# Keeping GpSimd's recorded order at the start of the main phase of a graph tensor product, with a wider window for one sort and edge numbers unpacked one unit later

## The chip, the cores and the metric

The kernel runs on one core of a Trainium2 chip. The metric is the device time of one execution in microseconds (us). The engines are PE (TensorE, matmuls; PEld is its weight load), DVE (VectorE), ACT (ScalarE), POOL (GpSimd) and SP (SyncE, which here only issues DMAs). L1043 means line 1043 of the kernel before the change.

## What is computed

There are N = 10000 nodes with 64 channels of 4 components each, and E = 640000 edges with random source and destination nodes. Each edge takes its source node's row of x, combines it with its own direction Y by the small tensor cg, scales it by a learned radial factor and adds the result to its destination node. At the end a 64 x 64 matrix mixes the channels.

```python
R = _silu(edge_feat @ w_rad)                              # (E, C)
xs = x[src]                                                 # (E, C, M)
tp = jnp.einsum('eci,ef,ifo->eco', xs, Y, cg)             # (E, C, M)
msg = R[:, :, None] * tp
agg = _segment_sum(msg.reshape(-1, C * M), dst, N).reshape(N, C, M)
return jnp.einsum('ncm,cd->ndm', agg, w_mix)
```

## The kernel before

The edges are sorted by destination on the chip, so that the messages of 32 neighbouring nodes can be summed by matmuls. The 32 nodes are a *bucket*, 18 buckets are a *group* (the last group has 7), and the edges are cut into three *parts* (32, 36.4 and 31.6 per cent). One part of one group is a *segment*; there are 3 x 18 = 54 of them, in the order of the list `self.segs`, which begins each part with the short group. The first segment therefore has 7 buckets, the second 18.

The first phase sorts part 0 by groups into DRAM. The main phase (`groups`) does three things at once:

- `messages` computes the messages. Its work is cut into 939 *units*, one bucket of one part each (5 or 6 tiles of 128 edges). A loop over k runs a pipeline of stages; `(gather, LG)` in its table means that the gather of unit k+5 stands in step k. `index` (L991 to L1000) takes the edge numbers `sidx` of a whole segment out of the sorted words `pay` on DVE, LI units ahead, at the first unit of each segment. `gather` (L1043) fetches 5 or 6 tiles of rows of x by indirect DMAs on POOL, five units ahead, into `xg`, which has seven buffers. `turn`, `turned`, `radial` and `silu` make the radial factors; `products` (L1096, DVE) multiplies `xg` by them, and `sums` (L1109, PE) adds a unit's messages up.
- `pass2` sorts one segment after the other by buckets. A segment is routed in *chunks* of 13 tiles: DVE makes `X` (L649), ACT and DVE make `oh`, PE multiplies them into the one PSUM bank `pr` (L682, L685), ACT copies the bank to `rt` (L690, five buffers), and POOL stores it with one indirect DMA, `bkt<-rt` (L696). While a segment is routed, `front` makes the tables of the next one. After the last chunk SP loads the segment's words back as `pay`, two buffers of them.
- `pass1` sorts the later parts by groups; its stores are `grp<-rt`.

`groups` weaves the three. A step v is a *quarter*: one of the four groups of stages of one unit. Segment i+1 must be sorted by quarter `ends[i]`; its sort is spread evenly from the end before. PE, DVE and ACT keep the order in which the instructions are recorded (`manual_schedule`). POOL and SP do not: a list scheduler with a cost model orders them at build time, and the engine then runs that order strictly.

```python
quarters = (((index, LI), (gather, LG), (fetch, 1), (turn, 2), (sums, 0), (silu, 1), (piece(0), 5), (piece(1), 4),
             (piece(2), 3)), ((evict, -1), (turned, 2), (spots, 1)),
            ((products, 1), (rest(0), 5), (rest(1), 4)), ((radial, 2), (full, -1)))
...
for k in range(-LI, n + 3):
```

Unit u is therefore gathered in step u-5 and multiplied in the third quarter of step u-1, and its segment's numbers are taken out in step u-LI. As step -LI is quarter 0, `index` of unit u always stands in quarter 4u, while everything else of `messages` moves by four quarters when LI moves by one.

Of the kernel before, what the change touches and what calls it, by code (L numbers as in the profile page):

```python
# [37 lines left out]
UT = 6  # L38
SPLIT = ((0.32, 5), (0.364, 6), (0.316, 6))
LG = 5  # L40
LI = 8
HEAVY = 4
BIG = 16384.0
FAR = 2097152.0
# [18 lines left out]
def weave(main, side, ratio):  # L63

    acc = 0.0
    for said in main:
        acc += ratio
        while acc >= 1.0:
            acc -= 1.0
            next(side, None)  # L70
        yield said
    yield from side


def run(gen):
    for _ in gen:
        pass


class Kernel:  # L80
# [868 lines left out]
    def messages(self):  # L949
# [63 lines left out]
        def piece(q):  # L1013
            def cast(k):

                at = block(k)
                if at is None:
                    return
                key, v, n = at
                if q == 0:  # L1020
                    E9[key] = ph.tile([P, HB * MT, 3, 3, 4], BF, name="e9", bufs=2)
                    ER[key] = ph.tile([P, HB * MT, 4], F, name="er", bufs=1)
                r = ER[key][:, :n] if q else v
                nc.scalar.activation(E9[key][:, :n, :, q, :], r.unsqueeze(2).to_broadcast([P, n, 3, 4]), AF.Copy)
            return cast
# [132 lines left out]
        def mixed(k, po):  # L1158
# [4 lines left out]
# [4 lines that stand above are left out]
        todo, po = [], None  # L1167
        for k in range(-LI, n + 3):
            for stages in quarters:
# [15 lines left out]
    def groups(self):  # L1185

        self.pay = {}
        sort, main, segs, NG = self.pass2(), self.messages(), self.segs, self.NG

        ends, u = [], 0  # L1190
        for k, g in segs:
            u += self.nb(g)
            ends.append(4 * max(u - LI - 3, ends[-1] // 4 + 1 if ends else 1))

        for k in range(1, len(SPLIT)):
            ends[k * NG - 1] -= 22

        later, at = [], 40
        for k in range(1, len(SPLIT)):
            end = max(ends[k * NG - 2] - 8, at + 1)  # L1200
            n = self.chunks(k)
            later.append((self.pass1(k, self.p1.NC // 2 * 2), at, end, HEAVY * n + 20 * (n / (self.p1.NC - 2) + 2)))
            at = end
        done = 0.0
        while segs[0] not in self.pay:
            next(sort)
        batch, got = self.batch(), None
        acc = 0.0
        i = start = 0
        for v in range(4 * u):  # L1210

            if later:
                first, at, end, n = later[0]
                due = "grp" in (self.held, self.pos, self.way)
                while done < n * (v + 1 - at) / (end - at) or due:
                    due = False
                    said = next(first, "end")
                    if said == "end":
                        later.pop(0)
                        done, self.sorted = 0.0, self.sorted + 1  # L1220
                    if said in ("held", "end"):
                        break
                    done += said or 1
            if i + 1 < len(segs):
                acc += self.pass2_steps(*segs[i + 1]) / (ends[i] - start)
                due = "bkt" in (self.held, self.pos, self.way)
                while (acc > 0.0 or v >= ends[i] or due) and segs[i + 1] not in self.pay:
                    due = False
                    said = next(sort)
                    if said == "held":  # L1230
                        break
                    acc -= said or 1
                if v >= ends[i] and segs[i + 1] in self.pay:
                    i, start, acc = i + 1, ends[i], 0.0
            elif got is None:
                if segs[-1] in self.pay:
                    run(sort)
                    self.remains()
                    got = "begun"
            elif got != "ready":  # L1240
                got = next(batch) or got
            next(main)
        assert not later
        for _ in main:
            if got != "ready":
                got = next(batch) or got
        while got != "ready":
            got = next(batch) or got
        run(batch)

    def chunks(self, part):
# [246 lines left out]
    def add(self, pay, si, dst, wx):  # L1498

        al = lambda nm, shape: self.ph.tile(shape, F, name=nm, bufs=1 + (nm == "oeq"))  # L1500
        xg = al("oxg", [P, OT, 64, 4])
        di = self.ph.tile([P, OT], I32, name="odi")
        self.reach(xg, si)
        run(self.join(al, pay, dst, di, [xg], wx))
        self.put(al, di, [xg])
# [37 lines left out]
    def run(self):  # L1543
        tile_pool, nc = self.tc.tile_pool, self.nc
        order = [self.NG - 1] + list(range(self.NG - 1))
        self.segs = [(k, g) for k in range(len(SPLIT)) for g in order]
        with tile_pool(name="p1", bufs=2) as self.ph, tile_pool(
                name="x1", bufs=1, space=bass.MemoryType.PSUM) as self.px:
            self.ways = 2
            self.rt_bufs, self.ls = 38, 8  # L1550
            self.lag, self.ahead, self.early = 2, 3, 1
            self.z = self.ph.tile([P, 2048], F, name="z", bufs=1)
            nc.gpsimd.memset(self.z, 0.0)
            self.consts()

            with self.tc.manual_schedule(engines={mybir.EngineType.SP}):
                first = self.pass1(0, 8)
                next(first)
                run(self.clear_groups(0, nc.gpsimd))
                for _ in range(40):  # L1560
                    next(first, None)
                while self.held:
                    next(first)
                self.weights()
                later = itertools.chain(self.clear_buckets(),
                                        *(self.clear_groups(k, nc.sync) for k in range(1, len(SPLIT))))
                run(weave(first, later, 0.185))
                self.sorted = 1
        with tile_pool(name="p2", bufs=2) as self.ph, tile_pool(
                name="x2", bufs=1, space=bass.MemoryType.PSUM) as self.px:  # L1570
            self.ways = 1
            self.rt_bufs, self.ls = 5, 4
            self.lag, self.ahead, self.early = 1, 2, 0
            self.p1.NC = 13
            self.p1.act = self.p2.act = 7
            with self.tc.manual_schedule(engines={mybir.EngineType.PE, mybir.EngineType.DVE,
                                                  mybir.EngineType.Activation}):
                self.groups()
        with tile_pool(name="p3", bufs=1) as self.ph, tile_pool(
                name="x3", bufs=1, space=bass.MemoryType.PSUM) as self.px:  # L1580
            self.ways = 2
            self.rest()
# [29 lines left out]
```

## Time and profile before

| what | us |
|---|---|
| time, median of 3 runs | 9988.29 |
| lowest and highest of these | 9968.19, 9993.34 |
| profiled execution, its own time | 9898.0 |
| its span, first to last instruction | 9896.2 |
| busy in the span: PE, DVE, ACT, POOL | 6566.6, 6947.1, 4425.9, 5961.4 |

The profiled execution is 0.9% faster than the median of the three runs, so durations are added up against 9898.0 and the result is carried over to the median by proportion. No engine is busy all the time: DVE leads with 70% of the span. In rows of the timeline the first number is the start in us from the span's start, the second the duration; `[14.01 <-remote]` is the engine's idle time before the instruction and what ended it. "issue" means that nothing shown ended the wait, "remote" that a semaphore did whose sender the profile cannot name. The starts and ends of matmuls are modelled.

### The profile page before, as it was taken

To read this page: it belongs to the slowest core of one execution; us is meant where nothing else is said; L and a number is where in the kernel's file an instruction comes from. 1 tells how busy PE (TensorE), PEld (TensorE's weight loads), DVE (VectorE), ACT (ScalarE), POOL (GpSimd) and SP (SyncE) were. 2 spreads that over 40 slices of the span, in tenths; PEclk is the share of its full clock that TensorE was granted. 3 is DMA by queue.
4 is the path that set the end of the run, shared out by engine and by line. 5 is a ranking of instruction groups with operands and counts; after the bars stand their busy time and mean duration, and the time that the engine had idled before them with its cause. 6 is when DMAs were issued, how large, how long until landed. Compare 5 with 4: busy or idle time off the path is not lost. (4 is left out here: it accounts for less than half of the span.)

```text
span 9896.2 us, 126276 instructions
## 1 busy us (share of the span) xinstructions
PE 6566.6 (66%) x41310; PEld 5222.8 (53%) x41310; DVE 6947.1 (70%) x13605; ACT 4425.9 (45%) x12394; POOL 5961.4 (60%) x6213
## 2 busy tenths in 40 slices
PE   6646666666666666666666666666666676667666
PEld 4435555555555555455555554555555555555555
DVE  8868878787876767767777777556666656666554
ACT  6845555555655444544544444433232323333221
POOL 4546666666666566566666666666556555555555
PEclk6568888887888777777777787777777777877878
DMA  6223333333333333333333333334334343344433
GB/s 206 85 63 101 102 102 100 102 103 101 99 103 101 97 108 104 94 105 102 101 103 105 98 101 101 100 107 112 111 111 119 107 120 112 112 116 114 115 108 94
DMA packets 694112, 1050.60 MB, mean 106 GB/s; under 512 B 272066, under 2 KB 501826, under 8 KB 693440
## 3 DMA queue, kind: packets, MB, share of 16 engines
q0 software_dynamic: 289104, 741.62, 26.3%
q1 hardware_dynamic: 404336, 300.81, 10.4%
q8 instruction: 325, 5.32, 0.2%
q14 instruction: 347, 2.84, 0.1%
HBM read 841.68 MB, written 213.95 MB: 107 GB/s over the span
## 5 line engine op out<-in xcount | busy, mean ns | idle before, releaser
L1043 POOL DMA_INDIRECT xg<-in_x_dram,sidx x5165 | 4934.7, 955 | 3054.0 <-issue 1354.6
L1109 PE MATMUL G<-S,xg 128*128 128x128 f32 x20660 | 3220.9, 315 | 550.4 <-issue 529.0
L1109 PEld LDWEIGHTS G<-S,xg 128*128 128x128 f32 x20660 | 2980.0, 226 | 639.1 <-issue 621.5
L682 PE MATMUL pr<-X,oh 128*128 128x320 bf16 (+2 forms) x10538 | 1888.6, 341 | 1083.5 <-ACT rt L690 486.6
L682 PEld LDWEIGHTS <-oh 128*128 128x128 bf16 x10538 | 1162.5, 117 | 1777.5 <-issue 1083.0
L1096 DVE TENSOR_TENSOR xg<-xg,pre 128x1536 f32<-128x1536 f32 (+1 forms) x939 | 1516.0, 1614 | 626.0 <-ACT pre L1072 421.7
L649 DVE TENSOR_TENSOR X<-dv,Wt 128x2080 f32<-128x2080 f32 (+4 forms) x854 | 1668.0, 1953 | 330.3 <-remote 216.8
L673 ACT ACTIVATE sq<-far,rowf 128x128 f32<-128x128 f32 x5702 | 1754.2, 394 | 2.7
L1072 ACT ACTIVATE pre<-pre 128x384 f32<-128x384 f32 (+1 forms) x939 | 423.6, 451 | 2042.2 <-issue 768.6
L1082 DVE TENSOR_TENSOR S<-dv,pay 128x768 f32<-128x768 f32 (+1 forms) x939 | 836.6, 891 | 510.3 <-remote 318.8
L674 ACT ACTIVATE oh<-sq,ones 128x896 bf16<-128x896 f32 (+2 forms) x854 | 899.9, 1054 | 23.9
L690 ACT ACTIVATE rt<-pr 128x320 bf16<-128x320 f32 (+1 forms) x854 | 349.5, 409 | 1197.2 <-remote 810.2
L696 POOL DMA_INDIRECT bkt<-rt,idx x437 | 439.3, 1005 | 409.3 <-issue 104.9
L1068 PE MATMUL pre<-wr,sT 108*128 108x192 bf16 x939 | 262.3, 279 | 634.1 <-ACT sT L1061 399.1
L1061 ACT ACTIVATE sT<-pre 108x256 bf16<-108x256 f32 x939 | 358.7, 382 | 531.9 <-remote 258.5
L1134 DVE TENSOR_TENSOR Gs<-old,G 128x256 f32<-128x256 f32 x313 | 130.3, 416 | 653.8 <-remote 410.1
L1154 PE MATMUL po<-wf,Gs 128*128 128x256 f32 (+2 forms) x1392 | 416.1, 454 | 138.4 <-ACT tot L433 83.3
L1068 PEld LDWEIGHTS <-sT 108*128 108x128 bf16 x939 | 98.3, 105 | 752.3 <-ACT sT L1061 453.5
L1056 PE MATMUL pre<-identb,e 128*108 128x128 bf16 x1878 | 305.8, 250 | 249.1 <-DVE xg L1096 160.2
L1056 PEld LDWEIGHTS <-e 128*108 128x108 bf16 x1878 | 247.5, 152 | 392.3 <-issue 301.3
L665 DVE TENSOR_TENSOR oh<-dv,pair 128x768 bf16<-128x768 bf16 (+3 forms) x852 | 446.8, 525 | 0.2
L1154 PEld LDWEIGHTS po<-wf,Gs 128*128 128x128 f32 (+2 forms) x1392 | 297.1, 220 | 228.1 <-ACT tot L433 86.5
(317 smaller groups left out, 6644.4 us busy)
## 6 DMA issues: line engine op xcount, KB each, us to landing
xg<-in_x_dram,sidx POOLq DMA_INDIRECT x5165
sums<-Gp SPq DMA_DIRECT2D x626, 128.0 KB
old<-sums SPq DMA_DIRECT2D x313, 256.0 KB
bkt<-z SPq DMA_DIRECT2D x26, 990.0 KB
pay<-bkt SPq DMA_DIRECT2D x68, 225.0 KB
ye<-in_Y_dram SPq DMA_DIRECT2D x103, 96.0 KB
ye<-in_edge_feat_dram SPq DMA_DIRECT2D x103, 96.0 KB
grp<-z SPq DMA_DIRECT2D x17, 580.0 KB
```

Of the source, the lines that this page charges most:

```text
L649: nc.vector.tensor_tensor(X[:, :m, :].rearrange("p t (s w) -> p t s w", w=W), msk.unsqueeze(3).to_broadcast([P, m, ps.r, W]), QD[c // Q][1 ...
L665: nc.vector.tensor_tensor(oh[:, :v, :].rearrange("p t (h k) -> p t h k", k=2), self.vb.rearrange("p (h k) -> p h k", k=2).unsqueeze(1).to_ ...
L673: nc.scalar.activation(sq[:, u, :], self.far, AF.Square, bias=to, scale=-1.0)
L674: nc.scalar.activation(oh[:, v:v + len(at), :], sq[:, :len(at), :], AF.Relu, bias=self.ones[:, 0:1], scale=-2.0)
L682: nc.tensor.matmul(pr[:, o:o + 2 * ps.rw], oh[:, u, :], X[:, u, :].bitcast(BF), start=(u == 0), stop=(not on and (u == m - 1 or u % TT == ...
L696: st = nc.gpsimd.indirect_dma_start(out=ps.dst, out_offset=bass.IndirectOffsetOnAxis(ap=idx[:, i:i + 1], axis=0), in_=rt[:, s * ps.rw:(s + ...
L1043: nc.gpsimd.indirect_dma_start(out=xg[:, t, :], out_offset=None, in_=self.x, in_offset=bass.IndirectOffsetOnAxis(ap=si[:, u:u + 1], axis=0))
L1056: nc.tensor.matmul(pre[:KR, 256 + 128 * h:384 + 128 * h], e[:, 36 * t:36 * t + KR], self.identb, start=True, stop=True)
L1082: nc.vector.tensor_tensor(S[:, :ut], self.eq[:, :ut].unsqueeze(3).to_broadcast([P, ut, NB, 4]), pb[:, :, 1:5].unsqueeze(2).to_broadcast([P ...
L1096: nc.vector.tensor_tensor(V, V, R.unsqueeze(3).to_broadcast([P, ut, 64, 4]), op=OP.mult)
L1109: nc.tensor.matmul(G[:, h].rearrange("p n f -> p (n f)"), v[:, 32 * h:32 * h + 32, :].rearrange("p c i -> p (c i)"), s.rearrange("p n f -> ...
L1154: nc.tensor.matmul(po[:nn, :256], Gs[:, h, f].rearrange("p b n -> p (b n)")[:, :nn], self.wf[:, h, f, :], start=(h + f == 0), stop=(h + f ...
```

## The change

Three edits, all in or for `groups`. LI goes from 8 to 7, so `index` stands seven units ahead. The first end, for the second segment's sort, becomes quarter 20 instead of quarter 4; the other ends stay, as the formula now has 11 where it had LI + 3. And `groups` yields once, at quarter 28, so that its caller can record everything up to there with POOL, too, in the recorded order.

```diff
-LI = 8
+LI = 7
...
-            ends.append(4 * max(u - LI - 3, ends[-1] // 4 + 1 if ends else 1))
+            ends.append(4 * max(u - 11, ends[-1] // 4 + 1 if ends else 5))
...
         for v in range(4 * u):
-
+            if v == 4 * LI:
+                yield
...
-            with self.tc.manual_schedule(engines={mybir.EngineType.PE, mybir.EngineType.DVE,
-                                                  mybir.EngineType.Activation}):
-                self.groups()
+            kept = {mybir.EngineType.PE, mybir.EngineType.DVE, mybir.EngineType.Activation}
+            groups = self.groups()
+            with self.tc.manual_schedule(engines=kept | {mybir.EngineType.Pool}):
+                next(groups)
+            with self.tc.manual_schedule(engines=kept):
+                run(groups)
```

On POOL, the main phase begins with the stores of the first segment's four chunks. In the order before, this follows (`xg<-in_x_dram` are gathers, five for each unit; `bkt<-rt` stores of one chunk each, eight for each whole segment of the first part):

```order
L696 DMA bkt<-rt,idx 136704x160 x4
L1043 DMA xg<-in_x_dram,sidx 128x256 x10
L696 DMA bkt<-rt,idx 136704x160
L1043 DMA xg<-in_x_dram,sidx 128x256 x8
L696 DMA bkt<-rt,idx 136704x160
L1043 DMA xg<-in_x_dram,sidx 128x256 x15
L696 DMA bkt<-rt,idx 136704x160
L1043 DMA xg<-in_x_dram,sidx 128x256 x2
L696 DMA bkt<-rt,idx 136704x160 x9
L1043 DMA xg<-in_x_dram,sidx 128x256 x5
```

On POOL at the same place, now:

```order
L696 DMA bkt<-rt,idx 136704x160 x4
L1043 DMA xg<-in_x_dram,sidx 128x256 x5
L696 DMA bkt<-rt,idx 136704x160 x2
L1043 DMA xg<-in_x_dram,sidx 128x256 x5
L696 DMA bkt<-rt,idx 136704x160 x3
L1043 DMA xg<-in_x_dram,sidx 128x256 x5
L696 DMA bkt<-rt,idx 136704x160 x3
L1043 DMA xg<-in_x_dram,sidx 128x256 x25
L696 DMA bkt<-rt,idx 136704x160
L1043 DMA xg<-in_x_dram,sidx 128x256 x5
```

Before, 35 gathers (units 0 to 6) stand around the first three of the second segment's eight stores; now 15 do, and units 3 to 7 follow the eighth store in one run of 25.

On DVE, the first `index` stands, before, behind the third segment's digits and the first `X` (L649) of the second segment; the rows begin with the places (`pair`, `slot`) of the second segment's first chunks:

```order
L633 TENSOR_SCALAR pair<-pos 128x104
L636 SCALAR_TENSOR_TENSOR slot<-pair,pos 128x52
L646 TENSOR_TENSOR dv<-dv,slot 128x208
L649 TENSOR_TENSOR X<-dv,Wt_7625 128x2080
L1276 TENSOR_TENSOR unp<-pay,sh 128x280
L1278 SCALAR_TENSOR_TENSOR pay<-unp,pay 128x35x8
L991 TENSOR_SCALAR sidx<-pay 128x35
```

On DVE now (line numbers behind L1193 are higher by one to four), the same `index` follows the first two rows on the third segment's words (L885, L886), ahead of its digits (L375, L381):

```order
L885 TENSOR_SCALAR dg_7892<-Wt_7888 128x102
L886 TENSOR_SCALAR dg_7892<-dg_7892 128x102
L1277 TENSOR_TENSOR unp<-pay,sh 128x280
L1279 SCALAR_TENSOR_TENSOR pay<-unp,pay 128x35x8
L991 TENSOR_SCALAR sidx<-pay 128x35
L993 TENSOR_SCALAR didx<-pay 128x35
L1000 SCALAR_TENSOR_TENSOR dlc<-didx,bn 128x35
L375 TENSOR_SCALAR two<-dg_7892 128x204
L381 TENSOR_TENSOR D_7895<-dv,two 128x720
```

So 10 rows of DVE (of L375, L381, L627, L633, L636, L646 and L649, the first `X` among them) that stood ahead of the first `sidx` now stand behind it. From unit 5 on, DVE's products stand between the sorts' rows as they stood before, but for one unit: what unit u had before it, unit u+1 now has (all but 14 of them, which differ by one chunk); PE's and ACT's rows do so from unit 11 on at the latest. Each `index` stands between the same sort rows as before, and so one product later.

## The prediction

> **What bounds the kernel now.** No engine is busy all the time, so I looked first for stretches in which none is, in the table of windows at the start of the main phase, the only place where the two kernels' POOL orders differ much. The numbers after each window's length are busy time and count by engine, then the granted PE clock, the DMA share and GB/s:
>
> ```profile
> core 0: us, PE busy (x) PEld busy (x) DVE busy (x) ACT busy (x) POOL busy (x), PEclk, DMA share, GB/s
> 575.00:600.00 25.00, 9.84 (x50) 5.49 (x49) 20.71 (x53) 12.84 (x35) 13.65 (x15) 0.64 0.23 66
> 600.00:625.00 25.00, 3.99 (x15) 2.02 (x15) 6.14 (x7) 4.05 (x11) 18.84 (x21) 0.57 0.36 102
> 625.00:650.00 25.00, 12.87 (x63) 7.33 (x63) 12.82 (x28) 16.10 (x43) 6.73 (x7) 0.70 0.12 34
> 650.00:675.00 25.00, 15.86 (x85) 8.90 (x85) 21.62 (x52) 15.36 (x44) 3.94 (x4) 0.79 0.18 47
> 656.00:762.00 106.00, 67.86 (x428) 53.16 (x426) 85.67 (x194) 52.10 (x149) 51.49 (x54) 0.79 0.32 89
> ```
>
> From 600 to 625 us DVE works 6.14 of 25 us and PE 3.99, while POOL issues. The waits of ACT between 575 and 640 us (total, times, longest) name the place, the copy of `pr` to `rt`:
>
> ```profile
> ACT rt L690 <- remote: 35.8, 2, 21.8
> ```
>
> The timeline of that stretch shows a chunk's last matmul early, and its copy late:
>
> ```profile
> 574.63 0.21 DVE L886 TENSOR_SCALAR dg<-dg 128x102 int32<-128x102 int32 x1
> ...
> 578.54 2.32 DVE L649 TENSOR_TENSOR X<-dv,Wt 128x2080 f32<-128x2080 f32 x1
> ...
> 582.08 1.00 POOL L1043 DMA_INDIRECT xg<-in_x_dram,sidx  x1 [10.72 <-DVE didx L993]
> ...
> 587.15 0.94 POOL L1043 DMA_INDIRECT xg<-in_x_dram,sidx  x1 [0.30 <-issue]
> 587.18 2.32 DVE L649 TENSOR_TENSOR X<-dv,Wt 128x2080 f32<-128x2080 f32 x1
> 589.00 0.30 PE L685 MATMUL pr<-rt,oh 128*128 128x320 bf16 x1
> ...
> 605.34 0.44 ACT L690 ACTIVATE rt<-pr 128x320 bf16<-128x320 f32 x1 [14.01 <-remote]
> ...
> 609.24 0.41 PE L685 MATMUL pr<-rt,oh 128*128 128x320 bf16 x1
> ...
> 613.63 0.95 POOL L1043 DMA_INDIRECT xg<-in_x_dram,sidx  x1 [0.30 <-issue]
> ...
> 624.89 0.95 POOL L1043 DMA_INDIRECT xg<-in_x_dram,sidx  x1 [0.30 <-issue]
> 631.25 0.44 ACT L690 ACTIVATE rt<-pr 128x320 bf16<-128x320 f32 x1 [21.83 <-remote]
> ```
>
> The second and third chunk of the second segment are copied 16 and 22 us after their last matmuls start (589.00 to 605.34, 609.24 to 631.25). Since there is only one `pr`, PE's next chunk waits too, then DVE. POOL issues gathers nearly without a pause from 582.08 to 624.89, and the wait ends 6 us after the last. That coincidence is all the trace says of the cause: `rt` has five buffers, which should not bind here, and the wait's sender is not named. Taking the stalls for the gathers' doing is the choice on which the forecast rests.
>
> **The change part by part.** It adds and removes no work: equally many gathers, stores, products and sort rows. I follow three positions in DVE's order, from which the rest is carried on unchanged: the second segment's last `X`, the first product, and a product behind the third segment's sort.
>
> ```profile
> 646.71 1.99 DVE L649 TENSOR_TENSOR X<-dv,Wt 128x1760 f32<-128x1760 f32 x1
> 648.73 0.34 SPq L869 DMA_DIRECT2D Wt<-gr  x1
> 652.27 0.25 DVE L885 TENSOR_SCALAR dg<-Wt 128x102 int32<-128x102 int32 x1 [3.16 <-DMA Wt<-gr]
> ...
> 656.61 2.33 DVE L649 TENSOR_TENSOR X<-dv,Wt 128x2080 f32<-128x2080 f32 x1
> ...
> 680.41 1.48 DVE L1096 TENSOR_TENSOR xg<-xg,pre 128x1280 f32<-128x1280 f32 x1
> ...
> 761.97 1.48 DVE L1096 TENSOR_TENSOR xg<-xg,pre 128x1280 f32<-128x1280 f32 x1
> ```
>
> *The second segment's sort.* Its last `X` stands at 646.71. Now three units' gathers stand around its stores instead of seven, in fives with two or three stores between; that is the pattern of one unit's gathers per chunk or two that the rest of the main phase has. I take both stalls away: 35.8 us. The ends are nothing gone, and 35.8; I stand at the upper one, because the run of 33 gathers (582.08 to 624.89, broken by two stores) no longer exists there: 15 are left, and none between the last three stores.
>
> *`index` ahead of the digits.* It now waits for `pay` before DVE has ten rows to hide the load under. The load is issued after this row:
>
> ```profile
> 572.93 0.50 SPq L933 DMA_DIRECT2D pay<-bkt  x1
> ```
>
> The nearest load on the same queue is that of `Wt`, issued at 648.73 and used at 652.27, 3.5 us. So `pay` is there at about 576.6 at the earliest, and DVE is free at 574.63 + 0.21 = 574.84: 1.8 us of waiting, with ACT, PE and the next tables behind it; the ends are 0 and twice the wait, 3.6. The last `X` then stands at 646.71 - 35.8 + 1.8 = 612.7.
>
> *The first product.* Everything of the messages stands one unit earlier against the sort, so unit 0's product now stands ahead of the third segment's first `X`. From the last `X` to that `X` is 656.61 - 646.71 = 9.9 us, most of it the load of `Wt`, which does not change; I allow 9.4 to the product's start, as it takes the place of that `X`'s last wait: 622.1, against 680.41 before. The product needs unit 0's gathers, which are the first five on POOL from about 582 on.
>
> *The third segment's sort.* From its first `X` (656.61) to the product of unit 10 (761.97) there are 105.4 us with eight chunks and 11 units. The same rows now lie between the products of units 0 and 11. DVE is busy for 85.67 of this (the window from 656 to 762); the rest has more of the same wait:
>
> ```profile
> 706.14 0.44 ACT L690 ACTIVATE rt<-pr 128x320 bf16<-128x320 f32 x1 [2.89 <-remote]
> ...
> 714.82 0.44 ACT L690 ACTIVATE rt<-pr 128x320 bf16<-128x320 f32 x1 [7.36 <-remote]
> ...
> 723.32 0.34 ACT L410 ACTIVATE colsgrp<-cnt 64x216 f32<-64x216 f32 x1 [7.51 <-remote]
> ```
>
> These three sum to 17.8. Here the run of 25 gathers that the change makes (units 3 to 7) falls in, which before was done earlier. The ends are DVE's busy time alone, 85.7 us, and the waits once more, 123.2. I take 105.4, as before: the mean need of POOL is the same over this stretch, and the 25 gathers at 0.95 + 0.30 us end about 31 us after 613, at 644. Unit 11's product then stands at 622.1 + 105.4 = 727.5. Unit 10's stood at this place at 761.97, so the order runs 34.5 us earlier, and one unit more is done.
>
> *One unit fewer at the end.* Behind the last sort only products are left, ten of them in this stretch:
>
> ```profile
> 9783.20 1.48 DVE L1096 TENSOR_TENSOR xg<-xg,pre 128x1280 f32<-128x1280 f32 x1
> ...
> 9847.40 1.48 DVE L1096 TENSOR_TENSOR xg<-xg,pre 128x1280 f32<-128x1280 f32 x1
> ```
>
> A unit costs (9847.40 - 9783.20)/10 = 6.4 us there, and one of them goes. The ends are 1.5 (only the product) and 9.6 (a unit amid the sort, 105.4/11).
>
> *POOL held behind stores.* In the recorded order a gather can wait for a store which waits for a copy. Unit 0's product is due at 622 and its gathers stand ahead of all eight stores; the last 25 end at about 644, while unit 3 is not due before 622 + 3 x 9.6 = 651. Nothing, then; if the stalls stay, the store of the eighth chunk comes 36 us later and so do these gathers, but the products as well.
>
> *`index` seven units ahead.* It keeps its place in the sort, but the gathers come a unit earlier against it. The segment with the least room in the trace:
>
> ```profile
> 5123.03 1.75 DVE L1096 TENSOR_TENSOR xg<-xg,pre 128x1536 f32<-128x1536 f32 x1 [2.14 <-ACT pre L1072]
> ...
> 5134.64 0.25 DVE L991 TENSOR_SCALAR sidx<-pay 128x108 int32<-128x108 int32 x1
> ...
> 5141.25 1.75 DVE L1096 TENSOR_TENSOR xg<-xg,pre 128x1536 f32<-128x1536 f32 x1
> ...
> 5148.24 0.98 POOL L1043 DMA_INDIRECT xg<-in_x_dram,sidx  x1 [1.95 <-PE pre L1069]
> ...
> 5203.80 1.75 DVE L1096 TENSOR_TENSOR xg<-xg,pre 128x1536 f32<-128x1536 f32 x1
> ```
>
> The first gather starts 13.4 us after `sidx` now (5148.24 - 5134.89). Measured from the products, `sidx` is ready 11.9 us after product 456; in the new order it will be so long after product 457, where POOL would want it after 7.0 (5148.24 - 5141.25): 4.9 us late. But that unit is multiplied at 5203.80, 55.6 us after its first gather, so the lateness stays on POOL. By the same sum only two more of the 52 later segments are late, by 1.1 and 1.2 us. Zero, with 7 us as the upper end.
>
> [...] DVE's `X` reads two SBUF tiles, and gathers are issued beside it: at 587.15 one takes 0.94 us while `X` runs from 587.18, and at 613.63, with DVE idle, one takes 0.95. [...]
>
> **Sum.** 34.5 + 6.4 = 41 us, 9898.0 - 41 = 9857 for the profiled execution. That execution is faster than the median (9988.29), so by proportion 9857 x 9988.29/9898.0 = 9947.
>
> **The rivals.**
>
> *The stalls are not the order's.* They stand under the second segment's sort, but waits of the same name come back at 706 to 723, where gathers stand in fives already. If late completions of PE come with any gathers, the 35.8 us stay: the last `X` at 648.5, and the gain is 41 - 36 = 5: 9983. If they go by the number of gathers beside the sort, 15 in place of 33, 16 of them stay and the gain is 25: 9963. Both are less than 0.3% (30 us), about what a measurement of this kernel can tell from no change. For it: those later rows, and a cause that the trace does not name. Against it: 14.0 and 21.8 us are two and three times those of 7.4 and 7.5.
>
> *More than the stalls.* With POOL's early run out of the way, the third segment's sort runs at DVE's pace: 85.7 in place of 105.4, gain 41 + 19.7 = 61: 9927. For it: 17.8 us of waits in that stretch. Against it: the run of 25 gathers falls into it.
>
> *`index` comes late everywhere, slower than before.* Each of 53 later segments would hold POOL at its first gather and the products behind it. The gain of 41 is used up, and a loss of 30 reached, from 71/53 = 1.3 us for each segment that gets through to DVE. At 4.9 us in each, the worst found, it is 260 - 41 = 219 us slower: 10207. For it: POOL has little rest (gathers 0.3 us apart), and a late start is made good slowly. Against it: the 55.6 us between gather and product.
>
> [...]
>
> **How the numbers follow.** The forecast has 0.56, the stalls that stay 0.28, the larger gain 0.09, late `index` 0.05, the waiting gathers 0.02. Faster by over 0.3%: of the forecast's 0.56 about nine tenths, since 41 is near 30 and the ends of its terms (17 us from the third segment's waits doubled) reach below it, and all of the 0.09: 0.60 in all. Within 0.3%: the remaining 0.06, the 0.28 and the 0.02, less a little for both sides: 0.34. Slower: 0.06. The range begins at the larger gain, 9927, less half of the 25 us between the lowest and highest run (9968.19 and 9993.34), 9915, and ends at the stalls that stay, 9983, plus as much, 9995; it leaves out late `index`. The likeliest case alone goes from 9938 (the third segment's 17.8 us of waits halved) to 9965 (doubled).
>
> **What would show it.** After: the sum of ACT's wait for `rt` between 575 and 625 falls from 35.8 to a few us, the last `X` of the second segment stands near 613, the first product near 622 and unit 11's near 727; the first gather of the segment that now has 5134.64 starts right after `didx`, and its product does not wait for a DMA. The forecast is wrong if ACT still shows two waits of over 10 us for `rt` there, or if the stretch from the first product to unit 11's is far from 105 us: the run of 25 gathers would then have taken the stalls along.

## The result, and the profile after

| | before | after |
|---|---|---|
| median of the runs, us | 9980.09 (4 runs, 9968.19 to 9993.34) | 9889.49 (4 runs, 9884.44 to 9890.23) |
| ratio, 95% interval | | 0.9908 (0.9891 to 0.9924) |
| profiled execution, its own time | 9898.0 | 9890.23 |

The change saves 91 us, 0.9%. That is more than twice the forecast's 41 us, and below the low end of its range (9915). The two profiles do not show those 91 us: their spans are 8 us apart, 9896.2 before, and after:

```profile
span 9888.4 us, 126272 instructions
```

The execution of before that was profiled was 82 us faster than the median of that kernel's runs. Later the same unchanged kernel had medians of 8196.22, 8197.28, 8204.44, 9882.26, 9974.25 and 9986.83 us on six chips, so chips differ by far more than the change. Each of these chips was used in one session only, so here a chip cannot be told from its session. Below, only kernels that ran on one and the same chip are compared, except where the text says otherwise.

At the start of the main phase the profile after shows the two stalls gone, as forecast. The table of windows (columns as before; 600 to 625 us had 6.14 us of DVE and 3.99 of PE):

```profile
core 0: us, PE busy (x) PEld busy (x) DVE busy (x) ACT busy (x) POOL busy (x), PEclk, DMA share, GB/s
575.00:600.00 25.00, 16.61 (x70) 8.23 (x71) 22.78 (x62) 17.69 (x48) 8.99 (x9) 0.60 0.17 45
600.00:625.00 25.00, 15.87 (x70) 8.76 (x70) 18.85 (x40) 16.77 (x45) 12.62 (x13) 0.67 0.26 78
625.00:650.00 25.00, 14.31 (x75) 8.69 (x74) 20.59 (x33) 12.75 (x32) 17.49 (x18) 0.70 0.41 107
```

ACT's waits from 575 to 640 us, where the copy of `pr` had waited 35.8 us for "remote":

```profile
ACT rt L690 <- PE pr L685: 4.9, 3, 3.4
...
ACT rt L690 <- remote: 2.5, 1, 2.5
```

The four places that the forecast follows: the second segment's last `X`, the first product, a late copy in the next sort, and the product of unit 11 (rows of DVE, and one of ACT):

```profile
617.85 1.99 DVE L649 TENSOR_TENSOR X<-dv,Wt 128x1760 f32<-128x1760 f32 x1
...
631.98 1.48 DVE L1096 TENSOR_TENSOR xg<-xg,pre 128x1280 f32<-128x1280 f32 x1
...
657.20 0.44 ACT L690 ACTIVATE rt<-pr 128x320 bf16<-128x320 f32 x1 [14.52 <-remote]
...
743.32 1.48 DVE L1096 TENSOR_TENSOR xg<-xg,pre 128x1280 f32<-128x1280 f32 x1
```

The last `X` came 29 us and the first product 48 us earlier than before. The product of unit 11 stands at 743.32, where unit 10's stood at 761.97: 18.7 us, not 34.5. A wait of 14.5 us has come up and ends at 657.20, in the run of 25 gathers that the change makes (20 of them start from 628.61 to 652.85).

### The profile page after: what moved, and what is told of

Same layout as the page of the kernel before. It is cut to its first block, busy times and chain, and to the rows that moved or that the text cites. A ratio compares the mean times of both kernels' runs of the same rounds, so it can differ in the third digit from the quotient of the medians.

```text
span 9888.4 us, 126272 instructions
## 1 busy us (share of the span) xinstructions
PE 6628.8 (67%) x41310; PEld 5252.3 (53%) x41310; DVE 6956.1 (70%) x13605; ACT 4422.7 (45%) x12394; POOL 5978.6 (60%) x6213
## 5 line engine op out<-in xcount | busy, mean ns | idle before, releaser
L649 DVE TENSOR_TENSOR X<-dv,Wt 128x2080 f32<-128x2080 f32 (+4 forms) x854 | 1668.4, 1954 | 284.5 <-remote 181.6
L1072 ACT ACTIVATE pre<-pre 128x384 f32<-128x384 f32 (+1 forms) x939 | 423.8, 451 | 2324.2 <-remote 1341.9
L690 ACT ACTIVATE rt<-pr 128x320 bf16<-128x320 f32 (+1 forms) x854 | 349.5, 409 | 1157.1 <-remote 631.4
L696 POOL DMA_INDIRECT grp<-rt,idx x283 | 285.1, 1008 | 208.3 <-issue 67.5
L696 POOL DMA_INDIRECT gr<-rt,idx x268 | 266.2, 993 | 236.9 <-ACT rt L690 145.4
```

Source lines behind the costliest of these rows:

```text
L649: nc.vector.tensor_tensor(X[:, :m, :].rearrange("p t (s w) -> p t s w", w=W), msk.unsqueeze(3).to_broadcast([P, m, ps.r, W]), QD[c // Q][1 ...
L696: st = nc.gpsimd.indirect_dma_start(out=ps.dst, out_offset=bass.IndirectOffsetOnAxis(ap=idx[:, i:i + 1], axis=0), in_=rt[:, s * ps.rw:(s + ...
L1072: nc.scalar.activation(RT[k], RT[k], AF.Silu)
```

## The experiments

`us` is the median, the ratio is to the kernel before on the same chip; each value of "before there" stands for one chip. The ratios are the recorded ones, which are not quotients of the two medians (those differ from them by up to 0.0012: 0.9892 for e9, 0.9920 for e8).

| run | what differs from the kernel before | us | before there | ratio (95% interval) |
|---|---|---|---|---|
| e1 | nothing | 8196.67 | 8196.22 | 1.0001 (0.9992 to 1.0010) |
| e2 | POOL kept in order only | 8190.83 | 8196.22 | 0.9993 (0.9984 to 1.0002) |
| e3 | edge numbers at 7 only | 8198.45 | 8196.22 | 1.0005 (0.9996 to 1.0014) |
| e4 | first end at quarter 20 only | 8195.95 | 8196.22 | 0.9999 (0.9990 to 1.0008) |
| e5 | the whole change | 9898.50 | 9986.83 | 0.9913 (0.9890 to 0.9936) |
| e6 | nothing | 9975.83 | 9974.25 | 1.0007 (0.9991 to 1.0023) |
| e7 | as e2 | 9975.93 | 9974.25 | 1.0000 (0.9988 to 1.0012) |
| e8 | as e3 | 9893.96 | 9974.25 | 0.9910 (0.9896 to 0.9925) |
| e9 | every sort due one unit later, edge numbers at 8 | 9775.57 | 9882.26 | 0.9904 (0.9879 to 0.9929) |
| e10 | only `index` one unit later | 9907.45 | 9882.26 | 1.0031 (1.0016 to 1.0045) |
| e11 | the start only (first end and POOL) | 9854.01 | 9882.26 | 0.9971 (0.9956 to 0.9986) |
| e12 | the whole change, edge numbers at 6 | 9864.46 | 9882.26 | 0.9988 (0.9970 to 1.0005) |
| e13 | the start and sorts due one unit later, edge numbers at 8 | 8206.52 | 8197.28 | 1.0010 (1.0001 to 1.0019) |
| e14 | as e13, last part two units later | 8223.09 | 8197.28 | 1.0036 (1.0022 to 1.0049) |
| e15 | every sort due two units later | 8210.78 | 8197.28 | 1.0017 (1.0007 to 1.0026) |
| e16 | the whole change | 8194.61 | 8197.28 | 0.9998 (0.9989 to 1.0007) |
| e17 | as e13 | 8206.82 | 8204.44 | 1.0003 (0.9994 to 1.0012) |
| e18 | the whole change | 8201.20 | 8204.44 | 0.9996 (0.9987 to 1.0006) |

**The kernel before once more, and each edit alone (e1 to e4).** e1 and e6 have no edit. The three single edits:

```diff
# e2: POOL kept, yield at quarter 4 * LI = 32
+            if v == 4 * LI:
+                yield
...
+            with self.tc.manual_schedule(engines=kept | {mybir.EngineType.Pool}):
+                next(groups)
# e3: edge numbers
-LI = 8
+LI = 7
-            ends.append(4 * max(u - LI - 3, ends[-1] // 4 + 1 if ends else 1))
+            ends.append(4 * max(u - 11, ends[-1] // 4 + 1 if ends else 1))
# e4: first end
-            ends.append(4 * max(u - LI - 3, ends[-1] // 4 + 1 if ends else 1))
+            ends.append(4 * max(u - LI - 3, ends[-1] // 4 + 1 if ends else 5))
```

> The kernel before, unchanged. Its profiled execution took 9898.0 us and its other runs 9968 to 9993 us, while the changed kernel had 9884 to 9890 us with and without a profile. Theory A (profile and runs differ in this kernel by chance, execution by execution): the new profile lies anywhere between 9890 and 9993, and the runs scatter over the same. Theory B (something fixed makes one execution of this kernel run in a faster way): times fall in two groups, near 9898 and near 9980, with nothing between. In both, a profile near 9980 will show where the 80 us lie: at the start of the main phase (the two stalls longer than 35.8 us), or spread over all units.

> Only POOL's order at the start of the main phase is changed: all eight stores of the second segment ahead of the first gather (12 stores, then 25 gathers); edge numbers 8 units ahead and the first end at quarter 4 as before. Forecast's theory (gathers beside the second segment's sort cause the two stalls): both go, the last X of the second segment stands near 611 instead of 646.7, and the profile gains up to 36 us, less what the gathers of the first units come late (they start at about 617 instead of 582, unit 0's product was at 680). Rival (late completions of PE come by themselves): the stalls stay, 9980 to 9990, no gain.

> Only the edge numbers 7 units ahead and with them everything else of the messages one unit earlier against the sort; POOL's first gathers and stores stand as before. Forecast's theory: the two stalls stay (35.8 us), the first product comes one unit earlier and a unit goes at the end: 6 us, near 9975. Rival (the gain is made in the whole main phase by the messages' standing one unit earlier): most of the 91 us, 9890 to 9920.

> Only the first end at quarter 20; POOL is free to order and puts 25 gathers ahead of the second segment's second store. Forecast's theory: the gathers still stand beside the sort, the stalls stay, and the store behind 25 gathers holds the copies: same as before or slower, 9970 to 10000. Rival (the spread alone takes the stalls away): a gain of 30 us or more.

They fell on a chip on which the kernel takes 8196 us, and none of them changes it by 0.1%. That chip's profile (e1) shows the same early gathers without the two stalls. POOL issues 33 of them from 549 to 592 us, and the table of windows and ACT's waits from 545 to 600 us show the same sort there:

```profile
545.00:570.00 25.00, 14.35 (x68) 8.07 (x68) 23.95 (x52) 18.86 (x55) 15.93 (x17) 0.64 0.27 78
570.00:595.00 25.00, 15.12 (x72) 8.38 (x70) 14.58 (x33) 13.73 (x35) 18.91 (x21) 0.77 0.42 124
```

```profile
ACT rt L690 <- DMA bkt<-rt,idx: 9.6, 1, 9.6
```

The copy waits once, 9.6 us, and for a store that stands behind gathers on POOL. No wait for "remote" is there. Over the whole run the copy's largest wait is for a named matmul:

```profile
ACT rt L690 <- PE pr L685: 213.3, 106, 5.7
```

In the kernel before on a chip of 9974 us (e6) it is this, in the whole run:

```profile
ACT rt L690 <- remote: 781.9, 140, 21.2
```

The semaphore that ends these "remote" waits can be read from the packed traces: it is one that only PE raises (in the first profile it ends all 138 of them at the copy). Its signals can therefore be counted against the (modelled) end of the last PE record before them that raises it. In e1 all but 2 of 4749 signals come within 0.05 us of that end, and those 2 stand at the program's end. In e6 only 1848 of 4295 do, and 1428 come more than 1.5 us after it. The ten traces from chips of 8196 to 8204 us are all like e1's; the ten from the slower chips, the first two profiles among them, have 1326 to 1458 such late signals each. So PE's completions come late on some of these chips, throughout the kernel (in the first profile before 58 times in the first ms and 129 to 172 times in each later one), and on others, those 2 at e1's end apart, not at all. e1's expectation, one kind of execution or another by chance, was wrong as to the large difference: the runs of the kernel before lie within 14 us of each other on the chip of e1 and within 89 on that of e6, and the two chips are 1778 us apart.

**The whole change on a second chip (e5).**

> The changed kernel, unchanged, beside the kernel before on one and the same chip. The kernel before took 8196 us on the chip of the first four experiments, against 9980 on the chip of the result, and its two stalls beside the second segment's sort were not there (the third X of the sort to the fourth: 33 us on the first chip, 7.4 there), with the same early gathers. Theory P (PE's late completions belong to the chip, and what the change takes away or moves is theirs): on a chip of 8196 us the change gives what its parts gave there, within 0.2% (8180 to 8200); on a chip of 9980 us it gives 0.5 to 1.2% again. Forecast's theory (the early gathers cause the loss, on any chip): 35 us or more, 8160 or less.

On a chip of 9987 us the gain is there again, 0.87%. Later, on two chips of 8197 and 8204 us, the whole change gave nothing (e16, e18). So the gain belongs to the chips with late completions, as theory P says, and the forecast's theory (35 us or more on any chip) is out. The change does not make completions less late: 1401 signals of PE come over 1.5 us late in the first profile before, and 1446 in the first after. What it changes is the work that waits for them.

**POOL's order and edge numbers, on a chip with late completions (e6 to e8).**

> The kernel before, for a second profile of it on a chip where it takes some 9980 us: the first profiled execution took 9898 us, 80 less than its other runs. If the 80 us lie at the start of the main phase, the first product stands about 80 us later than 680.4 in a profile of 9980, and everything behind it as much. If they are spread (PE's late completions, execution by execution), the first product stands within 20 us of 680 and the gap to the changed kernel's profile grows unit by unit from about 29 us at unit 10 to about 90 at the end.

> Only POOL's order at the start changed, on a chip of 9980 us (on one of 8196 us it gave 0.07%). If POOL's order is what counts: 0.6 to 0.9% (9890 to 9920). If the whole gain is the messages' standing one unit earlier against the sort through the main phase: none (9970 to 9990). Forecast's theory: the two stalls go, 30 to 36 us, about 9950.

> Only the edge numbers 7 units ahead, the messages one unit earlier against the sort, on a chip of 9980 us (none on one of 8196 us). If the main phase's order against the sort is what counts: most of the 90 us (9890 to 9920). If POOL's order at the start is: near 9975.

e6's profile (span 9987.0) has its first product at 682.52, 2 us from the first profile's, and its last 90 us later (9937.8 against 9847.4): the difference between the two profiles is not at the start, and grows along the run. e7 moved all gathers behind the second segment's eighth store. Its timeline (DVE, POOL, ACT, DVE):

```profile
616.88 1.99 DVE L649 TENSOR_TENSOR X<-dv,Wt 128x1760 f32<-128x1760 f32 x1
...
623.96 1.00 POOL L1043 DMA_INDIRECT xg<-in_x_dram,sidx  x1 [0.30 <-DVE D L381]
...
670.72 0.44 ACT L690 ACTIVATE rt<-pr 128x320 bf16<-128x320 f32 x1 [19.63 <-remote]
...
676.66 1.49 DVE L1096 TENSOR_TENSOR xg<-xg,pre 128x1280 f32<-128x1280 f32 x1 [1.90 <-DMA xg<-in_x_dram,sidx]
```

Both stalls are gone and the last `X` stands 32 us earlier than in e6 (648.9), as forecast. But 32 gathers now start between 623.96 and 664.16, and a stall of 19.6 us ends at 670.72; the first product is 6 us earlier, unit 10's 0.9 us, and the time the same as before. In all five profiles from such chips with the early run of 33 gathers (the first, e6, e8, e9, e10) two stalls stand beside it, 8.8 to 14.8 and 21.2 to 26.1 us long; moving the run moves the stall. How long it is does not follow from the run alone: e11 has the same run of 25 gathers behind the eighth store, and a single stall of 5.9 us.

e8, the edge numbers alone, has the whole 0.9%. From e6's profile to e8's, unit 10 comes 8.2 us earlier, unit 450 4.4, unit 626 (the first of the last part) 20.4 and the last unit 74.5: the gain lies far from the start, and most of it in the last part. The last product, in e6 and in e8:

```profile
9937.84 1.48 DVE L1096 TENSOR_TENSOR xg<-xg,pre 128x1280 f32<-128x1280 f32 x1
```

```profile
9863.36 1.48 DVE L1096 TENSOR_TENSOR xg<-xg,pre 128x1280 f32<-128x1280 f32 x1
```

**Which half of that edit, and the start alone (e9 to e12).** LI = 7 moves two things: `index` one unit later against everything else of the messages, and the messages one unit earlier against the sort. e9 and e10 have one of them each (except at the very start: the first end and the first quarter of `pass1` are fixed quarters in both). e11 is the changed kernel with LI = 8, its other lines untouched, and e12 with LI = 6.

```diff
# e9: the kernel before, LI = 8
-            ends.append(4 * max(u - LI - 3, ends[-1] // 4 + 1 if ends else 1))
+            ends.append(4 * max(u - 10, ends[-1] // 4 + 1 if ends else 1))
# e10: the kernel before, LI = 7
-            ends.append(4 * max(u - LI - 3, ends[-1] // 4 + 1 if ends else 1))
+            ends.append(4 * max(u - 12, ends[-1] // 4 + 1 if ends else 1))
# e11, e12: the changed kernel
-LI = 7
+LI = 8    # e11; 6 in e12
```

> The kernel before with every sort due one unit later (ends at u-10 in place of u-11), edge numbers still 8 units ahead: the messages stand one unit earlier against the sort, as in the changed kernel, but the edge numbers keep their distance from the messages. On a chip of 9980 us, where edge numbers at 7 alone gave 0.9%: if the messages' place against the sort makes the gain, 9885 to 9920; if the edge numbers' place does, 9965 to 9990. On a chip of 8196 us both say no change.

> Edge numbers at 7 with every sort due one unit earlier (u-12), so that messages and sort stand as before and only the edge numbers stand one unit later. If the messages' place against the sort makes the gain: 9970 to 9990 on a chip of 9980 us. If the edge numbers' own place (DVE rows, later first gathers of a segment) does: 9885 to 9920.

> The changed kernel with edge numbers at 8: only the spread of the second segment's sort and POOL's kept order. The first product came 50 us earlier and unit 10 to 30's 28 to 31 us earlier in the changed kernel's profiles. Forecast's theory: that stays to the end, 9945 to 9955 on a chip of 9980 us. If PE's pace sets the later units whatever the start: less than 10 us.

> The changed kernel with edge numbers at 6: the messages one more unit earlier against the sort. If less distance from sort to message is better as such, another 0.3 to 0.9% (9810 to 9860 on a chip of 9980 us). If 7 is a matter of how the rows of sort and messages happen to fall on PE, any sign, within 1% of the changed kernel; if the sorted words come too late, slower than the changed kernel with DVE waiting for a DMA at the first product of a segment.

The messages' place against the sort is worth 0.96% (e9), the start 0.29% (e11, 28 us), and the edge numbers' own later place costs 0.31% (e10). Their product, 0.9904 x 0.9971 x 1.0031 = 0.9906, is what the whole change gives (0.9908, 0.9913). That the parts add up in this way is not shown, though: e8 has the edits of e9 and e10 together and gave 0.9910 on another chip, where their product is 0.9935, and without the start it is already level with the whole change. The place against the sort carries the gain in both e8 and e9; the shares of the start and of the edge numbers were measured on one chip only. e12 has the messages two units earlier and the edge numbers nearer by two, and the gain is nearly gone: nearer is not better as such. Which of the two spoils it was not measured on such a chip.

e9 and e11 ran on one chip, and their messages stand one unit apart against the sort. Up to the product of unit 626, the last part's first, e9 is 4.2 us ahead, and at the last product 88.2 (the rows of e11, then of e9):

```profile
6825.15 1.75 DVE L1096 TENSOR_TENSOR xg<-xg,pre 128x1536 f32<-128x1536 f32 x1 [7.80 <-DMA bkt<-rt,idx]
...
9812.44 1.48 DVE L1096 TENSOR_TENSOR xg<-xg,pre 128x1280 f32<-128x1280 f32 x1
```

```profile
6820.92 1.75 DVE L1096 TENSOR_TENSOR xg<-xg,pre 128x1536 f32<-128x1536 f32 x1
...
9724.26 1.48 DVE L1096 TENSOR_TENSOR xg<-xg,pre 128x1280 f32<-128x1280 f32 x1
```

So 84 us come from the last part (of 88 between these two profiles; the medians of the two runs are 78 apart). In the first two e9 makes up the 42 us by which e11's first product is earlier (635.1 against 676.9) and these 4. DVE's waits in that part (total, times, longest) say where; e11's first:

```profile
DVE Gs L1134 <- remote: 390.0, 76, 12.9
DVE xg L1096 <- ACT pre L1072: 188.8, 54, 11.8
DVE Gs L1134 <- PE G L1109: 126.0, 45, 4.9
DVE pos L627 <- ACT pc L618: 100.1, 14, 8.3
DVE Gs L1134 <- PE pre L1056: 94.8, 16, 12.3
```

```profile
DVE Gs L1134 <- remote: 460.2, 95, 13.9
DVE Gs L1134 <- PE G L1109: 143.7, 60, 5.9
DVE Gs L1134 <- PE pre L1056: 103.9, 31, 8.1
DVE xg L1096 <- ACT pre L1072: 73.0, 32, 12.4
DVE Gs L1134 <- PE pr L685: 38.6, 8, 5.8
```

Two waits go: the product's for its radial factors (188.8 to 73.0) and the sort's tables' for the copy `pc` (100.1 to none), 216 us together. About 101 come back as longer waits at `Gs`, the sum over a bucket: with the smaller rows that are not shown they are 662 us in e11 and 763 in e9. All waits of DVE in that part add up to 1080 us in e11 and 991 in e9, 89 less, for a part that is 84 shorter; DVE is busy for the same time in it (1854.6 and 1858.5 us). The work of PE is the same; what changed is which rows of the sort stand ahead of the radial factors and the tables in PE's order. Signals of PE over 1.5 us late are not fewer (443 in e11, 489 in e9), but fewer of them follow the radial factors' last matmul (L1069: 124 and 85). That this is why the waits shrank is read from the traces and not tested, and why a completion is late is not settled.

**More of it (e13 to e18).** e13 and e17 leave the edge numbers at 8 and keep the rest, e14 gives the last part two units, e15 all parts two:

```diff
# e13, e17: the changed kernel with LI = 8
-            ends.append(4 * max(u - 11, ends[-1] // 4 + 1 if ends else 5))
+            ends.append(4 * max(u - 10, ends[-1] // 4 + 1 if ends else 5))
# e14: the same with
+            ends.append(4 * max(u - (10 if k < 2 else 9), ends[-1] // 4 + 1 if ends else 5))
# e15: the kernel before
-            ends.append(4 * max(u - LI - 3, ends[-1] // 4 + 1 if ends else 1))
+            ends.append(4 * max(u - 9, ends[-1] // 4 + 1 if ends else 1))
```

> The changed kernel with edge numbers at 8 and every sort due one unit later (u-10) instead: start and place of the messages as in the changed kernel, without the edge numbers' later place. If the three parts add up: 0.9904 x 0.9971 = 0.9875 of the kernel before on a chip with PE's late completions, 0.3% below the changed kernel on the same chip. If the edge numbers' 0.3% was only that chip's scatter: the same as the changed kernel, 0.991.

> As the one before, with the last part's sorts due two units later (u-9). With two units (edge numbers at 6) the last part's 17 whole segments took 2700 us, against 2723 with one and 2804 with none, while the first two parts lost 60 and 67 us. If the best place differs by part: 20 to 25 us below the one before (0.985 of the kernel before). If the last part only made up what the first two had delayed: the same as the one before or slower.

> The kernel before with every sort due two units later (u-9), edge numbers at 8, the start as before. If less distance from sort to message is better as such: below one unit's 0.9904, near 0.981. If each place has its own price, by how the sort's rows meet the messages' on PE: the first two parts slower than with one unit (2927 and 3212 us for 17 segments with two units, 2866 and 3145 with one), the last faster, in all 0.992 to 1.00.

> The changed kernel, beside the three others on the same chip: 0.9908 and 0.9913 so far on two chips; by the parts measured one by one 0.9904 x 1.0031 x 0.9971 = 0.9906.

> Edge numbers at 8, every sort due one unit later, the start as in the changed kernel. On a chip of 9880 to 9990 us, if the parts add up: 0.9875 of the kernel before, 0.3% below the changed kernel on the same chip; if the edge numbers' 0.3% was that one chip's: the same as the changed kernel. On a chip of 8196 us: 1.001 again.

> The changed kernel on the same chip: 0.9906 on a chip of 9880 to 9990 us, 0.9998 on one of 8196 us.

All six fell on chips of 8197 and 8204 us. There the whole change is nothing (0.9998, 0.9996), and a later sort costs: 0.1% or nothing (e13, e17), 0.17% (e15), 0.36% (e14). Whether e13's version beats the changed kernel on a chip with late completions, as the product of e9 and e11 (0.9875) would have it, was not measured. On the slower chips e9, 0.9904 with one number changed, is level with the whole change (0.9908 and 0.9913 on two others), within the intervals.

## Why the prediction was wrong

*The sum: 41 us forecast, 91 measured.* The step that failed is the one on the main phase, "One unit fewer at the end". It carried everything behind unit 11 on unchanged and gave the messages' place against the sort 6.4 us, the price of one unit. e9 gives it 0.96%, some 95 us on its chip. The term was mis-sized because the other 928 units were taken to run in the same time in the new order. The profile before held a sign: waits of ACT for "remote" do not end with the start. Three later ones were quoted, but the page has their sum for the copy alone, in its row of that copy:

```profile
L690 ACT ACTIVATE rt<-pr 128x320 bf16<-128x320 f32 (+1 forms) x854 | 349.5, 409 | 1197.2 <-remote 810.2
```

The change shifts the rows of the sort and of the messages against each other on PE, and such waits with them: in the profile after, the copy's are 631.4 us, and those of the radial factors' activation (L1072) 1341.9 where they were 686.5. That this shift, and not something else that goes with the messages' place, makes the gain is argued from the waits.

*The stalls under the second segment's sort: right in place, short-lived.* They go (35.8 to 2.5 us), and e7, which moves the gathers alone, shows that they go with them. The sender that the forecast could not name is PE: the two signals come 16.0 and 21.4 us after the end of its last record. The sort ends about where the forecast had it: the last `X` stands at 617.85 against 612.7. The rival that they are not the order's is half right: e1 has the gathers and no such stall, so they need a chip on which PE's completions are late as well.

*The stretch to unit 11: 111.3 us against 105.4.* The run of 25 gathers took a stall along (14.5 us), which the forecast named as what would make it wrong. Between the last `X` and the first product there are 14.1 us, not 9.4. The start as a whole gives 28 us by e11 (0.14 to 0.44% as an interval), with 34.5 forecast; that these lie so close rests on one chip, and by e8 the start adds nothing.

*`index` seven units ahead: nothing forecast, 0.31% slower measured.* In the segment that was worked out the mechanism went as forecast. It is the one with the least room, and in the profile after it has (DVE, POOL, DVE):

```profile
5122.18 0.25 DVE L991 TENSOR_SCALAR sidx<-pay 128x108 int32<-128x108 int32 x1
...
5128.30 0.98 POOL L1043 DMA_INDIRECT xg<-in_x_dram,sidx  x1 [0.30 <-issue]
...
5187.96 1.75 DVE L1096 TENSOR_TENSOR xg<-xg,pre 128x1536 f32<-128x1536 f32 x1 [6.43 <-ACT pre L1072]
```

Its first gather starts 5.9 us after `sidx` instead of 13.4, and its product waits for the radial factors, not for a gather. In e10 the products wait 80.6 us for gathers over the whole run, against 73.9 in e11 with the edge numbers at 8, on the same chip. Those 7 us are far less than the 25 us between e10 and the kernel before. What makes up the loss, which was measured on one chip only, stays open.

*The conversion.* Taking the sum against 9898 and carrying it to 9988 by proportion assumed that profile and runs differ evenly. They may come from different chips, or from the scatter of one: on the slower chips the kernel before's runs lie up to 93 us apart (9835.09 to 9928.33). No record of the first profile's chip settles it.

*The rivals.* POOL held behind stores cost nothing that shows: none of the first 14 products after waits for a gather. That gathers wait for `X`, to which the forecast gave 0.02, is shown by no run: in the first profile the 862 that start while an `X` runs take 0.95 us on average, the other 4303 take 0.96. In the segment followed, late `index` did not reach DVE. All three were forecast.

## What to carry to other kernels

When two streams of instructions are woven into one engine's order, the offset between them is a parameter of its own: shift it by one step with nothing else changed and measure, before pricing any visible stall, because here one unit's shift moved waits far behind it: 84 of the 88 us between e9 and e11 lie in the last part. Test each edit alone: here the edit that looked incidental carried the gain, and the two at the visible stalls gave a third of it at most. And compare a profile with the runs it stands for: 0.8% between them was nearly as large as the effect, so the profile could not stand for those runs.

## What the runs showed of the hardware

The same kernel took 8196 us on one chip and 9974 on another, with nearly the same DVE work (6926.2 us busy in e1, 6947.1 in the first profile before, from a slower chip too) and a granted PE clock of 0.849 in e1 against 0.780 in e6. On the slower chip semaphores from PE come up to 21 us after the modelled end of its matmuls in the waits of the copy of `pr`, 140 times over 1.5 us there alone (e6); on the faster chip not once among these waits (e1). The clock alone does not make that. In the first profile before, a chunk's 13 matmuls take 1.93 us together where the granted clock is 1.0, and 3.62 where it is 0.5:

```profile
587.23 1.93 PE L682 MATMUL pr<-X,oh 128*128 128x320 bf16 x13 [0.19 <-issue]
...
605.83 3.62 PE L682 MATMUL pr<-X,oh 128*128 128x320 bf16 x13 [16.53 <-issue]
```

The matmul behind them (L685) has 0.30 us in its record at 1.0 (median of 272) and 0.47 at 0.5 (median of 91). Together that is 1.9 us more for a chunk, not 16. In the first two profiles the granted clock takes the values 0.5 and 1.0 alone (501 stretches of each before, 515 after), and its shortest stretch is 3.413 us. No run here shows what holds the completions back.
